# Six 20-byte tiles move from behind the attention tiles to ahead of the weights, which shifts the weights and most attention tiles by 192 bytes in SBUF

## The chip, the cores and the metric

The kernel runs on one core of a Trainium2 chip. The metric is the device time of one execution in microseconds (us). The kernel before was timed three times; a fourth execution was profiled.

## The reference

Block-causal attention over 8 batches and 8 heads, followed by a two-layer feed-forward net with a leaky ReLU:

```python
B, H, S, D = 8, 8, 576, 64                      # q, k, v: float32
scores = np.matmul(q, k.transpose(0, 1, 3, 2)) / np.sqrt(D)
scores = np.where(pos_i // 64 >= pos_j // 64, scores, -1e9)
scores = scores - np.max(scores, axis=-1, keepdims=True)
attn = np.exp(scores)
attn = attn / (np.sum(attn, axis=-1, keepdims=True) + 1e-09)
x = np.matmul(attn, v)                          # -> (4608, 512)
h = x @ w_in                                    # 512 -> 2048
out = np.maximum(0.01 * h, h) @ w_out           # 2048 -> 512, float32
```

## The kernel before

The kernel keeps everything on one core: attention for 64 heads, and the feed-forward net on the attention's rows, 256 tokens (a chunk) at a time, 18 chunks in all. Each matrix product of the feed-forward net is done three times with operands split into a high and a low part in the four-byte format fp32r, to keep float32 accuracy: high times high, high times low, low times high. The names end in h and l for the two parts.

**The first layer** (`ffn1`, matmuls of line 805). For a chunk and a pair `u` of 128-wide slices of the 2048 hidden columns there are 2 groups of 12 matmuls. In each the weights `wih` or `wil` are the stationary operand, 128 columns that are loaded into the array ahead of the matmul, and the activations `xh` or `xl` are the moving operand, 256 columns that stream through. 18 chunks, 8 pairs, 2 groups and 12 terms make 3456 matmuls, which write `p_h` in PSUM.

**The second layer** (`ffn2`, line 824). Here it is the other way round: the activations `gh` and `gl` are stationary, 128 columns, and the weights `woh` and `wol` are moving, 512 columns. For a chunk and a pair there are 2 groups of 6, in all 1728 matmuls, which write `p_o`.

**Attention.** The scores of a head (line 487) have queries `qs` as stationary and keys `kh`, `kl` as moving operand. The product with the values (line 641) has `vs` as stationary and the transposed probabilities `pth` (high) and `ptl` (low) as moving operand. The tiles `qs`, `kh` and `kl` exist twice, and successive heads take the one and the other (`z = i % 2`). Between the two products come the row maxima `nm` (VectorE, line 505), the exponentials with their row sums `sums` (ScalarE, line 514), the reciprocals `rec` (VectorE, lines 528 and 529), the division, and a transposition, which from the third batch on goes over DRAM (`turn`, `way`, `ptm`).

**Order.** A planner in the kernel (`class Plan`) simulates all operations with fixed costs, chooses an engine for those that can run on several, and writes them out; each engine then runs its list in order, with semaphores between engines. The planner's costs know nothing of addresses. The matmuls of the two layers are strewn between those of attention, so that TensorE has work while the softmax runs elsewhere; the last chunks run when attention is over.

**Memory.** The tiles of the pool `const` are laid out one behind the other in the order in which `fixed(...)` asks for them, each rounded up to a multiple of 32 bytes per partition. A tile's address is the same in each partition. In the kernel before, the first is `wih`, and the six tiles `nm`, `sums` and `rec` (two of each, 5 float32 values, 20 bytes per partition) come behind `vs` and ahead of `xr`, `g`, `gh`, `gl`, `xh`, `xl` and `ob`.

Of the kernel before, what the change touches and what calls it, by code (L numbers as in the profile page):

```python
# [9 lines left out]
F32 = mybir.dt.float32  # L10
# [7 lines left out]
P = 128  # L18
# [3 lines left out]
NT = 5  # L22
# [204 lines left out]
def attention_ffn(ctx: ExitStack, tc: tile.TileContext, qk: bass.AP, v: bass.AP, w_in: bass.AP, w_out: bass.AP, out: bass.AP):  # L227
# [33 lines left out]
    def fixed(shape, dt, name, n=None, pool=const):  # L261
        if n is None:
            return pool.tile(shape, dt, name=name)
        return [pool.tile(shape, dt, name=f"{name}{i}") for i in range(n)]
# [3 lines left out]
    def identity(pool):  # L268
        one = fixed([P, P], F32, "ident", None, pool)
        make_identity(nc, one)  # L270
        return one

    wih = fixed([P, ND, DFF], F32R, "wih")
    wil = fixed([P, ND, DFF], F32R, "wil")
    woh = fixed([P, NF, DM], F32R, "woh")
# [24 lines left out]
    kh = fixed([P, S], F32R, "kh", 2)  # L300
    kl = fixed([P, S], F32R, "kl", 2)
    vs = fixed([P, NT, 2 * D], F32R, "vs")
    nm = fixed([P, NT], F32, "nm", 2)
    sums = fixed([P, NT], F32, "sums", 2)
    rec = fixed([P, NT], F32, "rec", 2)
    for y in range(2):
        nc.gpsimd.memset(sums[y], 1.0)
    xr = [fixed([P, ND, S], F32, "xr0"), None]
# [603 lines left out]
```

## Time and profile before

| what | value |
|---|---|
| median of 3 runs | 1119.18 us (1118.76 to 1122.32) |
| the profiled execution, its own time | 1119.52 us |
| its span, first to last instruction | 1117.7 us |
| TensorE busy | 1083.7 us, 97% of the span, 6896 matmuls |
| weight loads busy (beside the matmuls) | 971.3 us, 87% |
| VectorE, ScalarE, GpSimd busy | 762.2, 708.3 and 475.5 us |
| granted TensorE clock, mean | 0.997 |

Busy time is the time in which at least one instruction of an engine is under way by the profile. The matmuls overlap each other in it (a matmul of the first layer is listed with some 0.28 us, and the next one starts about 0.115 us later), so what a matmul costs is read from one start to the next, not from its listed duration. The chain of waits, followed back from the last instruction, merges neighbouring pieces of one line and gives the length of each such stretch: divided by the number of its matmuls it gives the pace.

### The profile page before, as it was taken

To read this page: it belongs to the slowest core of one execution; us is meant where nothing else is said; L and a number is where in the kernel's file an instruction comes from. 1 tells how busy PE (TensorE), PEld (TensorE's weight loads), DVE (VectorE), ACT (ScalarE), POOL (GpSimd) and SP (SyncE) were. 2 spreads that over 40 slices of the span, in tenths; PEclk is the share of its full clock that TensorE was granted. 3 is DMA by queue.
4 is the path that set the end of the run, shared out by engine and by line. 5 is a ranking of instruction groups with operands and counts; after the bars stand their busy time and mean duration, and the time that the engine had idled before them with its cause. 6 is when DMAs were issued, how large, how long until landed. Compare 5 with 4: busy or idle time off the path is not lost.

```text
span 1117.7 us, 20595 instructions
## 1 busy us (share of the span) xinstructions
PE 1083.7 (97%) x6896; PEld 971.3 (87%) x6896; DVE 762.2 (68%) x2115; ACT 708.3 (63%) x1696; POOL 475.5 (43%) x501
## 2 busy tenths in 40 slices
PE   5799999999999999999999999999999999999998
PEld 4578788888889989999999998999989998999997
DVE  6998978879878777877666678787877776400000
ACT  7998767767777766655655566676677765322222
POOL 3444244545544444433443345455444445422221
PEclk9999999999999999999999999999999999999999
DMA  7766421157766656564445456656676655200000
GB/s 235 231 201 198 133 95 61 61 173 208 199 198 189 201 170 201 176 170 147 128 151 148 128 171 185 203 171 203 176 205 185 194 156 160 59 20 19 1 20 19
DMA packets 96810, 166.24 MB, mean 149 GB/s; under 512 B 10176, under 2 KB 79808, under 8 KB 96704
## 3 DMA queue, kind: packets, MB, share of 16 engines
q1 hardware_dynamic: 96704, 164.93, 50.0%
q8 instruction: 54, 0.88, 0.3%
q14 instruction: 52, 0.43, 0.1%
HBM read 111.41 MB, written 53.48 MB: 148 GB/s over the span
## 4 chain that ended last, share of the span: by engine, by line
PE 69%; DVE 16%; ACT 6%; DMA 4%; issue 2%; SPq 1%; POOL 0%; ACTq 0%; DVEq 0%; POOLq 0%
PE p_h L805 27%; PE p_o L824 27%; PE p_t L641 6%; PE p_s L487 6%; DVE nm L505 4%; ACT prow L514 4%; DVE turn L703 2%; DVE qs L464 2%; DMA way<-turn 2%; DMA ptm<-way 2%; PE p_t L568 2%; PE p_s L481 1%; DVE p_s L498 1%; DVE ptl L253 1%; SPq L720 1%
## 5 line engine op out<-in xcount | busy, mean ns | idle before, releaser
L805 PE MATMUL p_h<-xh,wih 128*128 128x256 f32 x1152 | 327.0, 284 | 1.6 <-DVE xh L244 1.6
L805 PE MATMUL p_h<-xl,wih 128*128 128x256 f32 x1152 | 323.1, 280 | 1.0 <-DVE xl L253 0.9
L805 PE MATMUL p_h<-xh,wil 128*128 128x256 f32 x1152 | 322.5, 280 | 0.0
L254 POOL TENSOR_TENSOR gl<-g,gh 128x512 fp32r<-128x512 f32 x110 | 149.4, 1359 | 368.2 <-ACT gh L243 317.7
L805 PEld LDWEIGHTS p_h<-xl,wih 128*128 128x128 f32 x1152 | 218.6, 190 | 11.6 <-DVE xl L253 1.4
L805 PEld LDWEIGHTS p_h<-xh,wih 128*128 128x128 f32 x1152 | 217.9, 189 | 11.8 <-DVE xh L244 1.8
L805 PEld LDWEIGHTS p_h<-xh,wil 128*128 128x128 f32 x1152 | 219.4, 190 | 0.0
L514 ACT ACTIVATE prow<-p_s,nm 128x192 f32<-128x192 f32 (+4 forms) x308 | 160.0, 525 | 74.1 <-DVE nm L505 73.4
L812 ACT ACTIVATE g<-p_h 128x512 f32<-128x512 f32 x144 | 86.0, 597 | 174.6 <-PE p_h L805 168.4
L824 PE MATMUL p_o<-woh,gh 128*128 128x512 f32 x576 | 183.1, 399 | 0.0
L824 PE MATMUL p_o<-wol,gh 128*128 128x512 f32 x576 | 179.7, 393 | 0.0
L824 PE MATMUL p_o<-woh,gl 128*128 128x512 f32 x576 | 179.1, 392 | 0.0
L703 DVE STREAM_TRANSPOSE turn<-prow 128x384 f32<-128x384 f32 (+3 forms) x384 | 143.9, 401 | 33.2 <-POOL prow L542 24.0
L542 POOL TENSOR_SCALAR prow<-prow,rec 128x320 f32<-128x320 f32 (+4 forms) x142 | 77.3, 557 | 148.7 <-DVE rec L529 106.7
L505 DVE TENSOR_REDUCE nm<-p_s 128x1 f32<-128x192 f32 (+4 forms) x308 | 137.4, 480 | 3.3
L824 PEld LDWEIGHTS p_o<-woh,gl 128*128 128x128 f32 x576 | 108.2, 188 | 24.8
L824 PEld LDWEIGHTS p_o<-wol,gh 128*128 128x128 f32 x576 | 108.2, 188 | 24.4
L544 ACT ACTIVATE prow<-prow,rec 128x192 f32<-128x192 f32 (+4 forms) x124 | 75.5, 614 | 48.6 <-DVE rec L529 48.4
L243 ACT CAST gh<-g 128x512 fp32r<-128x512 f32 x139 | 86.1, 620 | 22.0 <-PE p_o L824 20.5
L254 POOL TENSOR_TENSOR ptl<-ptm,pth 128x448 fp32r<-128x448 f32 x83 | 97.6, 1193 | 3.6 <-ACT pth L243 3.6
L243 ACT CAST pth<-ptm 128x448 fp32r<-128x448 f32 x191 | 94.4, 564 | 5.4 <-DMA ptm<-way 4.9
L824 PEld LDWEIGHTS p_o<-woh,gh 128*128 128x128 f32 x576 | 90.9, 188 | 3.6 <-issue 0.4
(81 smaller groups left out, 1655.0 us busy)
## 6 DMA issues: line engine op xcount, KB each, us to landing
way<-turn SPq DMA_DIRECT2D x192, 224.0 KB, 3.0
ptm<-way SPq DMA_DIRECT2D x192, 224.0 KB, 4.3
qk_in<-in_qk SPq DMA_DIRECT2D x56, 576.0 KB, 3.8
v_stage<-in_v SPq DMA_DIRECT2D x56, 160.0 KB, 2.3
out<-ob SPq DMA_DIRECT2D x35, 256.0 KB, 2.5
raw<-in_w_in SPq DMA_DIRECT2D x32, 256.0 KB, 3.3
raw<-in_w_out SPq DMA_DIRECT2D x32, 256.0 KB, 3.4
qk_in<-in_qk SPq DMA_DIRECT2D x8, 320.0 KB, 3.6
```

Of the source, the lines that this page charges most:

```text
L243: one = lambda: nc.scalar.copy(dst(), src())
L254: ("POOL", pool2(n), lambda: nc.gpsimd.tensor_sub(dst(), one(), two())),
L487: go = lambda ap=ap, cols=cols, kk=kk, k0=k0, k1=k1, first=first, last=last: nc.tensor.matmul(ap, qs[z][:, cols], kk[:, k0:k1], start=firs ...
L505: [("DVE", dve(kw[t]), lambda t=t, ap=ap, flat=flat: nc.vector.tensor_reduce(nm[z][: qn[t], t : t + 1], ap[: qn[t]], axis=AX.X if flat els ...
L514: nc.scalar.activation(o, ap[: qn[t]], AF.Exp, bias=nm[z][: qn[t], t : t + 1], scale=1.0, accum_out=sums[z][: qn[t], t : t + 1])
L542: ("POOL", pool1(kw[t]), lambda: nc.gpsimd.tensor_scalar(p(), p(), by, 1.0, op0=ALU.mult, op1=ALU.mult)),
L544: ("ACT", act(kw[t], True), lambda: nc.scalar.mul(p(), p(), by)),
L641: nc.tensor.matmul(to, vs[:, j, :], src, start=start, stop=stop)
L703: nc.vector.transpose(dst, src.rearrange("p (s b i) -> p s b i", b=4, i=32))
L805: nc.tensor.matmul(hh[:, i, :], w[:, d, f * P : (f + 1) * P], x[:, d, :], start=k == 0, stop=k == len(terms) - 1)
L812: add([("ACT", act(512), lambda: nc.scalar.activation(g, hh, AF.Prelu, alpha=0.01))], rank, [("h", z)], ["g"])
L824: nc.tensor.matmul(p_o[m], a[:, i, m * P : (m + 1) * P], w[:, 2 * u + i, :], start=u == 0 and k == 0, stop=u == NU - 1 and k == 5,)
```

## The change

The three lines that allocate the six small tiles stand ahead of those for the weights. Nothing else is touched.

```diff
         make_identity(nc, one)
         return one
 
+    nm = fixed([P, NT], F32, "nm", 2)
+    sums = fixed([P, NT], F32, "sums", 2)
+    rec = fixed([P, NT], F32, "rec", 2)
     wih = fixed([P, ND, DFF], F32R, "wih")
     wil = fixed([P, ND, DFF], F32R, "wil")
     woh = fixed([P, NF, DM], F32R, "woh")
...
     vs = fixed([P, NT, 2 * D], F32R, "vs")
-    nm = fixed([P, NT], F32, "nm", 2)
-    sums = fixed([P, NT], F32, "sums", 2)
-    rec = fixed([P, NT], F32, "rec", 2)
     for y in range(2):
         nc.gpsimd.memset(sums[y], 1.0)
```

In the built programs every instruction of every engine stands in the same place, with the same shape, before and after; only addresses differ. Six tiles of 32 bytes make 192 bytes, by which everything between the old and the new place moves up. What lies behind the old place stays. The start of a tile within a line of 512 bytes (its address modulo 512) is then:

| tile | role on TensorE | before | after |
|---|---|---|---|
| `wih`, `wil` | stationary, first layer | 384 | 64 |
| `xh`, `xl` | moving, first layer | 64 | 64 |
| `gh`, `gl` | stationary, second layer | 64 | 64 |
| `woh`, `wol` | moving, second layer | 384 | 64 |
| `qs`, `kh`, `kl`, heads with z = 0 | scores | 384 | 64 |
| `qs`, `kh`, `kl`, heads with z = 1 | scores | 128 | 320 |
| `pth` | moving, values | 384 | 64 |
| `ptl` | moving, values | 64 | 64 |
| `vs` | stationary, values | 384 | 64 |
| `prow0_1` to `prow0_4`, `qk_in0` | transposition, loads | 384 | 64 |
| `xr`, `g`, `ob`, `turn`, `ptm`, `v_stage` | copies and transfers | 64 or 320 | the same |
| `nm`, `sums`, `rec` | softmax | 384 to 32 | the same |

Slices of `wih`, `wil`, `woh`, `wol`, `xh`, `xl`, `gh`, `gl` and `vs` that a matmul reads start at multiples of 512 bytes within their tile, so the table holds for them too. All of these starts are multiples of 32 bytes, those of the large tiles multiples of 64.

## Prediction

> **What bounds the kernel.** I read the head of the page first, then the chain that ended last, then the timeline of TensorE.
>
> ```profile
> span 1117.7 us, 20595 instructions
> PE 1083.7 (97%) x6896; PEld 971.3 (87%) x6896; DVE 762.2 (68%) x2115; ACT 708.3 (63%) x1696; POOL 475.5 (43%) x501
> PEclk9999999999999999999999999999999999999999
> PE 69%; DVE 16%; ACT 6%; DMA 4%; issue 2%; SPq 1%; POOL 0%; ACTq 0%; DVEq 0%; POOLq 0%
> ```
>
> TensorE (PE) is busy 97% of the span at the full granted clock, and 69% of the chain is its matmuls. From 250 us on it has no gaps worth naming, and every other engine waits for it or works beside it. I therefore ask one question of the change: does a matmul follow its predecessor sooner or later when its operands start elsewhere? In the stretch from 440 to 640 us the chain is made of matmuls alone, and a count of the two layers' matmuls in the same window gives their mean pace:
>
> ```profile
> by line: PE p_o L824 41.5%; PE p_h L805 40.9%; PE p_s L487 9.1%; PE p_t L641 8.7%
> ...
> 440.00:640.00 200.00, 90.52 (x705) 89.72 (x706) 1.00 0.51 148
> ...
> 440.00:640.00 200.00, 91.62 (x360) 63.91 (x360) 1.00 0.51 148
> ```
>
> The first row is the chain in that window by line; the other two are the window's matmuls of line 805 (705) and of line 824 (360), with busy time and count, then the weight loads, the clock, DMA. First layer: 40.9% of 200 us is 81.8 us, over 705 matmuls 116.0 ns each. Second layer: 41.5% is 83.0 us, over 360 matmuls 230.6 ns each. These two means, times 3456 and 1728, are 400.9 and 398.5 us, together 71% of the time; the change moves one operand of every one of these 5184 matmuls.
>
> **How steady that pace is.** The chain's merged stretches show that identical matmuls do not always run alike:
>
> ```profile
> 446.53 0.53 PE p_s L487 x4
> 447.06 1.37 PE p_o L824 x6
> 448.43 1.41 PE p_h L805 x12
> 449.85 1.39 PE p_o L824 x6
> ...
> 454.40 1.12 PE p_s L487 x8
> ...
> 461.07 0.53 PE p_s L487 x4
> ...
> 468.94 1.12 PE p_s L487 x8
> ...
> 753.15 5.65 PE p_h L805 x48
> ...
> 1062.93 2.75 PE p_o L824 x12
> 1065.68 2.75 PE p_h L805 x24
> ```
>
> Columns: start, length, line, number of matmuls. The first layer runs at 5.65 / 48 = 117.7 ns per matmul in one stretch and at 2.75 / 24 = 114.6 in another. The second runs at 1.39 / 6 = 231.7 and at 2.75 / 12 = 229.2. Inside the quick stretch the starts one by one are
>
> ```profile
> 1066.22 0.28 PE L805 MATMUL p_h<-xh,wih 128*128 128x256 f32 x1
> ...
> 1068.15 0.28 PE L805 MATMUL p_h<-xh,wil 128*128 128x256 f32 x1
> 1068.26 0.39 PE L824 MATMUL p_o<-woh,gh 128*128 128x512 f32 x1
> ```
>
> with 18 first-layer matmuls from the first of these rows to the last: 2.04 us / 18 = 113.3 ns. So the first layer has a quick pace of 113.3 and a slow one of 117.7, and the mean of 116.0 lies between. Address and shape are the same in both, so the pace is set by how the streams of weight load and matmul fall against each other in time. This is the only place where I see a price that the addresses could touch.
>
> **The change part by part.** It removes and adds no instruction, moves none in any engine's list, adds no wait and touches no queue. What is left is where operands start.
>
> 1. *First layer, stationary operand.* `wih` and `wil` go from 384 to 64 in the 512-byte line, `xh` and `xl` stay at 64. Before, weights and activations start 320 bytes apart in the line, afterwards alike. Bounds: all matmuls at the quick pace give 3456 x (116.0 - 113.3) = 9.3 us less; all at the slow pace give 3456 x (117.7 - 116.0) = 5.9 us more.
> 2. *Second layer, moving operand.* `woh` and `wol` go from 384 to 64, `gh` and `gl` stay at 64. Bounds: 1728 x (230.6 - 229.2) = 2.4 us less, 1728 x (231.7 - 230.6) = 1.9 us more.
> 3. *Attention.* Queries and keys move together, so what lies alike there stays alike; `pth` and `vs` also move together, and `ptl`, which stays, becomes like `vs`. I take 0: the pair that changes is priced in the rows below at 0 to 5 ns for 280 matmuls, at most 1.4 us.
> 4. *Loads into `qk_in0`* (every second head in the first two batches and all heads after). The transfer is issued ahead and takes 3.8 us at the median:
>
> ```profile
> qk_in<-in_qk SPq DMA_DIRECT2D x56, 576.0 KB, 3.8
> ```
>
> A head takes about 14.5 us in the window above (scores start at 439.86, 454.40 and 468.94 by the chain's rows), which covers a transfer much slower than this. 0.
> 5. *VectorE, ScalarE, GpSimd* on shifted tiles: they hide under TensorE (68%, 63% and 43% busy), and the small tiles keep their place in the line. 0.
>
> For the value between the bounds of points 1 and 2 the trace has pairs that already lie alike. The scores have keys and queries at 384 and 384 for one head, at 128 and 128 for the next. Four of them, 288 columns each, take 0.53 us both at 446.53 and at 461.07, and eight take 1.12 us at 454.40 and at 468.94: where in the line the pair starts (256 bytes further) changes nothing that these rows can show. Their pace is 0.53 / 4 = 132.5 ns, that is 0.460 ns per column, and 117.7 / 256 is also 0.460: a pair that lies alike runs at the slow pace of a pair that does not. But four matmuls are the start of a group, and the first layer too starts slowly:
>
> ```profile
> 1075.15 0.28 PE L805 MATMUL p_h<-xh,wih 128*128 128x256 f32 x1
> ...
> 1075.63 0.28 PE L805 MATMUL p_h<-xl,wih 128*128 128x256 f32 x1
> ...
> 1076.54 0.62 PE L824 MATMUL p_o<-woh,gh 128*128 128x512 f32 x2
> ```
>
> Its first four matmuls take 0.48 us, 0.469 ns per column, the other eight 0.91 us, 0.444. So like against like position, pairs that lie alike are no slower, and at most 2% quicker for four matmuls. The second comparison is the product with the values, where the stationary `vs` (384) meets `pth` (384, alike) and `ptl` (64, 320 bytes apart as in the first layer), in listed durations:
>
> ```profile
> L641 PE MATMUL p_t<-ptl,vs 128*128 128x512 f32 x104 | 43.8, 421 | 0.1
> L641 PE MATMUL p_t<-pth,vs 128*128 128x512 f32 x104 | 43.3, 416 | 0.0
> ...
> L641 PE MATMUL p_t<-ptl,vs 128*128 128x256 f32 x48 | 13.5, 282 | 0.0
> L641 PE MATMUL p_t<-pth,vs 128*128 128x256 f32 x48 | 13.5, 280 | 0.0
> ...
> L805 PE MATMUL p_h<-xh,wih 128*128 128x256 f32 x1152 | 327.0, 284 | 1.6 <-DVE xh L244 1.6
> L805 PE MATMUL p_h<-xl,wih 128*128 128x256 f32 x1152 | 323.1, 280 | 1.0 <-DVE xl L253 0.9
> ```
>
> The unlike pair is 5 ns (512 columns) and 2 ns (256 columns) longer. Two kinds of first-layer matmul whose operands lie the same way differ by 4 ns in the same listing, merely by their place in the group, so I read the 2 to 5 ns as place too.
>
> The sum is therefore 0 for each point, with the bounds 9.3 + 2.4 + 1.4 = 13.1 us down and 5.9 + 1.9 = 7.8 us up. The profiled execution took 1119.52 us, 1.8 us more than its span and 0.3 us more than the median of the runs, 1119.18. Forecast: 1119.2 us for the median. No change means within 0.3%, 3.4 us, about what a measurement of this kernel can tell (its three runs spread by 3.6 us).
>
> The two paces are the row; a rule stands against them. The Trainium skill, page "TensorE: Matmul & The Clock Gate", section "Step-by-step: what each phase is for", says that TensorE reads moving operand and weights through two independent SBUF ports, so that loading the next weights takes nothing from the running matmul. By it, how the two lie to each other is worth exactly 0 us and both bounds fall away; it speaks against the change, and raises my chance for no change. The trace agrees only in part: with the ports free of each other a group of equal matmuls should have one pace, and the rows give 113.3 and 117.7 ns.
>
> **The rivals.**
>
> *Faster: the group settles at once.* If lying alike ends what makes the streams disturb each other, the start of each group and the slow stretches go, and both layers run at 113.3 and 229.2 ns: 9.3 + 2.4 us, 1107.8 us. For it: the mean lies nearer to the slow pace (2.7 ns above the quick one, 1.7 below the slow one), so there is more to win than to lose, and the two `ptl` rows point this way (2 ns on 3456 and 5 ns on 1728 matmuls would be 15.5 us, 1104.0). Against it: the scores lie alike and do not run at 0.443 ns per column.
>
> *Slower: the streams lock in the slow pace.* Weight load and matmul now start at the same offset, and if each step of the load meets the matmul's step in the same place, every group stays at 117.7 and 231.7 ns: 5.9 + 1.9 us, 1127.3 us. It decides once more than 43% of what could be lost is lost (3.4 of 7.8 us). For it: the scores' 0.460 ns per column, equal to the slow pace. Against it: the same pace heads each group of the unlike pair as well.
>
> *A part of either.* The means could shift by less than 3.4 us: this counts as no change.
>
> **How the numbers follow.** No change, because addresses at this grain do not matter or the two paces mix as before: 0.46. Faster by the first rival, in whole or large part: 0.31. Slower by the second: 0.23. The two rivals end near 1107.8 and 1127.3, and most of a partial effect lies inside; I take 1107 to 1127, which leaves out the 15.5 us reading of `ptl`, a wholly new pace and a full lock a little beyond the bound, together under 2 in 10. The likeliest case alone is 1116 to 1122.5.
>
> **What would show it.** Right: the stretches of line 805 in the chain again show both 113 and 117.7 ns, with 116.0 and 230.6 as means from 440 to 640 us. The faster rival: all long stretches of line 805 at 2.72 us per 24, the first four of a group included. The slower one: the last chunks, after attention, at 2.83 us per 24 instead of 2.75. Wrong altogether would be a pace outside 113.3 to 117.7, which would mean that the common part of the pace, and not only its spread, hangs on addresses.

## The result and the profile after

The changed kernel is slower: 1129.79 us median of 7 runs (1127.29 to 1132.70) against 1122.08 us of the kernel before on the same chip (1116.27 to 1123.68), ratio 1.0077 with a 95% interval from 1.0053 to 1.0100. The forecast of no change was wrong, and the median lies 2.8 us above the range. The kernel before took 2.9 us more in these runs than the 1119.18 us from which the forecast started; against its own base the change costs 7.7 us. The profiled execution took 1128.09 us with a span of 1126.3 us, 8.6 us longer than before.

The head of the page and its chain, after:

```profile
span 1126.3 us, 20595 instructions
PE 1094.0 (97%) x6896; PEld 981.6 (87%) x6896; DVE 760.7 (68%) x2115; ACT 708.4 (63%) x1696; POOL 473.7 (42%) x501
...
PE p_h L805 30%; PE p_o L824 29%; PE p_t L641 7%; PE p_s L487 6%; ACT prow L514 0%; DVE nm L505 0%; DVE xr L610 0%; ACT g L812 0%; ACT xr L243 0%; ACT g L243 0%; DVE p_s L498 0%; DVE xr L661 0%; ACT gh L243 0%; ACTq L243 0%; ACTq L514 0%
```

TensorE is busy 10.3 us longer, with the same instructions at the same clock, and idle 1.7 us less (34.0 us before, 32.3 after), which makes the 8.6 us of the span; the other engines' busy time is as before or a little less. The stages tell where. Busy time by engine before 250 us and from there to the end, first of the kernel before, then after (after the length of the stretch: busy time and count of TensorE, weight loads, VectorE, ScalarE and GpSimd, then the granted clock, the DMA share and GB/s):

```profile
0.00:250.00 250.00, 225.07 (x1366) 189.16 (x1366) 210.94 (x613) 196.05 (x529) 105.81 (x146) 0.99 0.50 154
250.00:1118.00 868.00, 858.68 (x5532) 782.15 (x5530) 551.24 (x1502) 512.21 (x1169) 369.69 (x355) 1.00 0.51 147
```

```profile
0.00:250.00 250.00, 225.11 (x1375) 189.86 (x1376) 211.02 (x618) 197.15 (x532) 106.10 (x148) 0.99 0.50 155
250.00:1127.00 877.00, 868.88 (x5522) 791.76 (x5521) 549.72 (x1498) 511.21 (x1166) 367.57 (x354) 1.00 0.50 145
```

In the first 250 us, where TensorE also waits for others, its busy time stays at 225.1 us. After that its busy time grows by 10.2 us. The window from 440 to 640 us of the kernel after, read as in the prediction (chain by line, then the count of line 805, then of line 824):

```profile
by line: PE p_h L805 41.6%; PE p_o L824 41.0%; PE p_s L487 8.9%; PE p_t L641 8.7%
...
440.00:640.00 200.00, 91.93 (x696) 90.44 (x696) 1.00 0.50 145
...
440.00:640.00 200.00, 90.51 (x355) 63.30 (x356) 1.00 0.50 145
```

First layer: 83.2 us over 696 matmuls, 119.5 ns each, before 116.0. Second layer: 82.0 us over 355, 231.0 ns, before 230.6. The first layer has 2988 of its matmuls after 250 us; 3.5 ns on each is 10.5 us, enough for the whole loss. (Line 805's own busy time in that part goes from 385.1 to 395.0 us, 9.9 us more; line 824's grows by 0.9 us.) The chain's long stretches show that this is no shift between the two paces seen before, but a third one:

```profile
756.49 5.75 PE p_h L805 x48
...
984.53 5.75 PE p_h L805 x48
990.28 2.75 PE p_o L824 x12
...
1073.33 2.87 PE p_h L805 x24
```

5.75 / 48 = 119.8 ns and 2.87 / 24 = 119.6 in each of these stretches, where the kernel before has stretches at 114.6 and at 117.7 ns. One group of the last chunks in the timeline:

```profile
1077.43 0.28 PE L805 MATMUL p_h<-xh,wih 128*128 128x256 f32 x1
1077.54 0.28 PE L805 MATMUL p_h<-xl,wih 128*128 128x256 f32 x1
1077.66 0.28 PE L805 MATMUL p_h<-xh,wil 128*128 128x256 f32 x1
...
1078.74 0.28 PE L805 MATMUL p_h<-xh,wil 128*128 128x256 f32 x1
1078.86 0.40 PE L824 MATMUL p_o<-woh,gh 128*128 128x512 f32 x1
```

The first matmul is followed after 0.11 us; the other eleven take 1.32 us, 120 ns each. The group of the kernel before in the prediction started slowly and then settled at 113.3. That holds beyond these rows: of the 233 first-layer runs of 12 matmuls or more from 250 us on, taken from the fifth start to the eleventh, 151 settle at 113 to 114 ns and 82 at 118 before, and all 233 at 119 to 120 after.

### The profile page after: what moved, and what is told of

Same layout as the page of the kernel before. It is cut to its first block, busy times and chain, and to the rows that moved or that the text cites. A ratio compares the mean times of both kernels' runs of the same rounds, so it can differ in the third digit from the quotient of the medians.

```text
span 1126.3 us, 20595 instructions
## 1 busy us (share of the span) xinstructions
PE 1094.0 (97%) x6896; PEld 981.6 (87%) x6896; DVE 760.7 (68%) x2115; ACT 708.4 (63%) x1696; POOL 473.7 (42%) x501
## 4 chain that ended last, share of the span: by engine, by line
PE 72%; ACT 0%; DVE 0%; issue 0%; ACTq 0%
PE p_h L805 30%; PE p_o L824 29%; PE p_t L641 7%; PE p_s L487 6%; ACT prow L514 0%; DVE nm L505 0%; DVE xr L610 0%; ACT g L812 0%; ACT xr L243 0%; ACT g L243 0%; DVE p_s L498 0%; DVE xr L661 0%; ACT gh L243 0%; ACTq L243 0%; ACTq L514 0%
## 5 line engine op out<-in xcount | busy, mean ns | idle before, releaser
L805 PE MATMUL p_h<-xl,wih 128*128 128x256 f32 x1152 | 326.4, 283 | 1.0 <-DVE xl L253 0.9
L805 PE MATMUL p_h<-xh,wil 128*128 128x256 f32 x1152 | 326.7, 284 | 0.0
L805 PEld LDWEIGHTS p_h<-xh,wih 128*128 128x128 f32 x1152 | 220.2, 191 | 11.8 <-DVE xh L244 1.8
```

The lines of the kernel that those rows point to most:

```text
L805: nc.tensor.matmul(hh[:, i, :], w[:, d, f * P : (f + 1) * P], x[:, d, :], start=k == 0, stop=k == len(terms) - 1)
```

## The experiments

The theory after the result: in the first layer the weight load of the next matmul runs beside the matmul that streams, both read SBUF, and the pace hangs on the distance between their start addresses (weights minus activations), with some period. Rivals: the weights' own place in the line counts; or something else that moved (small tiles, attention tiles, transfers). In all kernels below the distance is given modulo 512: before 320, after 0. The second layer, where the activations are loaded and the weights stream, has the same distance with the other sign.

**First set: period, or own place.** Four layouts. `d256`: the change, and one of the six large attention tiles (`kl1`, 2304 bytes) also ahead of the weights.

```diff
+    nm = fixed([P, NT], F32, "nm", 2)
+    sums = fixed([P, NT], F32, "sums", 2)
+    rec = fixed([P, NT], F32, "rec", 2)
+    kl1 = fixed([P, S], F32R, "kl1")
     wih = fixed([P, ND, DFF], F32R, "wih")
...
-    kl = fixed([P, S], F32R, "kl", 2)
+    kl = [fixed([P, S], F32R, "kl0"), kl1]
```

> Weights start 256 bytes behind the activations in the 512-byte line (320 against 64). Two bands: if the pace hangs on the distance modulo 128 or 256, this is the changed kernel again: first layer 119.4 ns, second 231.5 ns, +0.7% against before. If it hangs on the distance modulo 512 (only alike is bad): first layer 116 ns or less, within 0.3% of before or quicker. If the weights' own place decides: any pace.

Measured: ratio 1.0076 (1.0049 to 1.0104) to the kernel before, the loss of the change once more. First layer 41.6% of 200 us over 696 matmuls, 119.5 ns; long stretches as after the change:

```profile
475.56 4.32 PE p_h L806 x36
580.08 2.87 PE p_h L806 x24
```

So 256 bytes more of distance change nothing, and "alike within a line of 512 bytes" is not what counts.

`d064`: the kernel before with `kl1` alone ahead of the weights.

> Weights 64 bytes behind the activations (128 against 64). Distance modulo 128 or 256: the same residue as before (320), so first layer 116.0 ns, second 230.6 ns, within 0.3% of before. Distance modulo 512: a pace of its own, near that of alike if nearness counts (119 ns). Weights' own place: 128 is the same modulo 256 as 384 before, so 116 ns as well.

Measured: ratio 1.0022 (1.0004 to 1.0041). First layer 41.6% over 717, 116.0 ns. Its stretches have the pattern of the kernel before, quick and slow in the same places:

```profile
758.85 5.65 PE p_h L806 x48
984.54 5.46 PE p_h L806 x48
1027.24 2.75 PE p_h L806 x24
```

The interval of its time lies just above 1 all the same. Its runs also had a lower granted clock, 0.991 in the mean against 0.993 of the kernel before beside it, so the 0.2% can't be put down to the layout.

`d448`: `nm` and `sums` ahead of the weights, `rec` in its old place.

> Weights at 0, activations at 64: distance 448. Modulo 128 this is 64 as before: 116.0 and 230.6 ns, within 0.3% of before. Modulo 256 it is 192, a residue neither kernel has: then a pace of its own is possible, between 113.3 and 120 ns. Modulo 512 likewise.

Measured: ratio 1.0057 (1.0023 to 1.0090). First layer 41.5% over 707, 117.4 ns; second 40.2% over 343, 234.4 ns. Residue 192 is another pace than residue 64, so the period is not 128. Together with the two equal pairs (0 and 256, 64 and 320) it is 256 bytes, as far as these pairs show.

`d320_moved`: the kernel before with an unused tile of 128 bytes ahead of everything.

```diff
+    fixed([P, 32], F32, "gap")
     wih = fixed([P, ND, DFF], F32R, "wih")
```

> The kernel before with 128 unused bytes ahead of the weights: weights at 0, activations at 192, their distance 320 as before. If only the distance counts: the same time as before within 0.3%, 116.0 and 230.6 ns. If the start of the weights or of the activations in the line counts by itself: another pace; as weights at 0 are shared with the run at distance 448, the two would then be alike.

Measured: ratio 1.0005 (0.9984 to 1.0026), first layer 41.5% over 716, 115.9 ns. Everything moved and nothing happened; with weights at 0 this kernel and `d448` differ by 1.5 ns in the first layer. The weights' own place is out as the cause.

**Second set: which layer, and the other distances.** `second_only`: the three lines stand between `wil` and `woh`.

```diff
     wil = fixed([P, ND, DFF], F32R, "wil")
+    nm = fixed([P, NT], F32, "nm", 2)
+    sums = fixed([P, NT], F32, "sums", 2)
+    rec = fixed([P, NT], F32, "rec", 2)
     woh = fixed([P, NF, DM], F32R, "woh")
```

> The small tiles stand between wil and woh: only the second layer's weights (and the attention tiles) come to lie like the activations, the first layer's stay 320 bytes apart. If each layer pays for the distance of its own two operands: first layer 116.0 ns as before, second 231.6 ns as changed, and most of the loss is gone: below +0.3%. If something else moved with the small tiles (their own place, the attention tiles): first layer at 119.4 ns as well, +0.7%.

Measured: ratio 1.0041 (1.0024 to 1.0057), half of the loss, somewhat more than expected. The window:

```profile
by line: PE p_o L824 41.6%; PE p_h L805 40.9%; PE p_s L487 8.8%; PE p_t L641 8.7%
...
440.00:640.00 200.00, 90.75 (x704) 89.75 (x705) 1.00 0.51 146
...
440.00:640.00 200.00, 91.91 (x360) 63.99 (x360) 1.00 0.51 146
```

First layer 116.2 ns, second 231.1: the pace follows each layer's own distance. But in the last chunks the first layer, whose addresses are those of the kernel before, now runs at its slow pace throughout:

```profile
1023.07 2.83 PE p_h L805 x24
1067.84 2.83 PE p_h L805 x24
```

That is 117.9 ns against 114.6 before. Counted as above, 62 of the 233 runs settle at 113 to 114 ns and 171 at 118, where it was 151 and 82. Attention has ended in these last chunks, so among TensorE's operands there only the second layer's weights lie elsewhere: what the second layer's group leaves behind bears on which of its two paces the first layer's group settles at.

`d384` (`nm` ahead of the weights), `d352` (one of the six small tiles ahead) and `d288` (32 unused bytes behind `vs` in the kernel before):

> Distance 384, that is 128 modulo 256, the residue no run has yet. If nearness to alike is what costs, this is the quickest: first layer 113.3 to 115 ns, second 229 ns, up to 0.9% faster than before. If pace goes smoothly from residue 64 (116.1 and 231.1 ns) to 192 (117.6 and 233.9 ns): between them, 116.9 and 232.5 ns, +0.3%.

> Distance 352, 96 modulo 256: half a step of 64. If the grain is 64 bytes, this is like residue 64 or 128, 116.1 ns. If it is 32 bytes or finer: between the paces of 64 and 128, a pace of its own.

> The kernel before with 32 unused bytes ahead of the activations: distance 288, 32 modulo 256. Smooth in the distance: between alike (119.4 ns) and residue 64 (116.1 ns), so near 117.8 ns and +0.3%. Grain of 64 bytes: the pace of 0 or that of 64, 119.4 or 116.1 ns.

Measured: 1.0110 (1.0084 to 1.0136), 1.0099 (1.0076 to 1.0122) and 1.0074 (1.0053 to 1.0095). Residue 128, the farthest from alike, is not the quickest but nearly the slowest (119.3 ns): neither of the two bands expected for it came, and nearness to alike is no measure. `d352` has a pace of its own (118.1) between its neighbours, and `d288` 118.2, near the smooth guess, though its time is more than twice the +0.3% expected, as the second layer slowed too. Steps of 32 bytes matter. In `d288` the weights, the queries, keys and `vs` stay where they are in the kernel before, so a loss of this size comes about without any of these tiles moving.

**Third set: nothing moved but the load's start.** `w_back_after` is the changed kernel with one edit in the first layer: the load reads 128 columns that begin 48 columns (192 bytes) earlier, save for the first of the 16 slices of the hidden columns, which can't begin earlier. The kernel then multiplies with other weights, so its output is not the reference's; only the address is of interest.

```diff
+                f0 = max(0, f * P - 48)
                 nc.tensor.matmul(
-                    hh[:, i, :], w[:, d, f * P : (f + 1) * P], x[:, d, :], start=k == 0, stop=k == len(terms) - 1
+                    hh[:, i, :], w[:, d, f0 : f0 + P], x[:, d, :], start=k == 0, stop=k == len(terms) - 1
```

> The changed kernel, every tile in its place, but the first layer's weight loads read 48 columns (192 bytes) further back, so with other weights than the reference's (15 of 16 slices; the first stays). Their distance to the activations is then 64 modulo 256, as before. If the pace hangs on where the weight load starts against the moving operand: first layer 116.3 ns, second 232 ns as changed, time within 0.3% of before, or up to 0.4% above as with the second layer's tiles alone. If it hangs on anything else that moved (attention tiles, small tiles, transfers): 119.4 ns and +0.8% stay.

Measured: ratio 1.0032 (1.0014 to 1.0050) to the kernel before. The window:

```profile
by line: PE p_o L825 40.9%; PE p_h L806 40.6%; PE p_t L641 9.4%; PE p_s L487 9.2%
...
440.00:640.00 200.00, 90.03 (x696) 88.82 (x696) 1.00 0.52 149
```

116.7 ns, near the 116.3 expected. `w_back_before` is the same edit with 16 columns in the kernel before.

> The kernel before, every tile in its place, but the first layer's weight loads read 16 columns (64 bytes) further back (wrong weights in 15 of 16 slices). Distance 256, so 0 modulo 256. Same theory: first layer 119.2 ns, about 9 us in the part after 250 us, +0.8%, with nothing allocated elsewhere. Rival: 116.2 ns and the time of before.

Measured: ratio 1.0107 (1.0078 to 1.0136). The window:

```profile
by line: PE p_h L806 42.0%; PE p_o L825 39.7%; PE p_t L641 9.5%; PE p_s L487 8.8%
...
440.00:640.00 200.00, 92.66 (x705) 91.06 (x703) 1.00 0.52 151
```

119.1 ns, as expected. With every tile in its place, starting the weight load elsewhere takes more than half of the loss away in the one kernel and makes it in the other.

The slice that keeps its address is a control within the same execution. In `w_back_before`, a first-layer group of that slice starts at 1077.07 us, and the group of the next slice, whose loads are shifted, follows without a gap:

```profile
1077.77 0.28 PE L806 MATMUL p_h<-xh,wih 128*128 128x256 f32 x1
...
1078.45 0.28 PE L806 MATMUL p_h<-xh,wih 128*128 128x256 f32 x1
1078.57 0.28 PE L806 MATMUL p_h<-xl,wih 128*128 128x256 f32 x1
...
1079.89 0.63 PE L825 MATMUL p_o<-woh,gh 128*128 128x512 f32 x2
```

The last six matmuls of the slice that stayed take 0.68 us, 113.3 ns each. From the second matmul of the shifted slice on, eleven take 1.32 us, 120 ns each. In all its 15 groups after 250 us the slice that stayed settles at 113 to 118 ns here, the other fifteen at 119 to 120; in `w_back_after` it is the other way round, 119 to 120 for the slice that stayed and 113 to 118 for the others.

That settles the cause of the first layer's pace: the distance between the start of the weight load and that of the streaming operand. The small tiles, the attention tiles and the transfers have no part in this pace that these runs could show. Of the loss in time, 0.3% stays in `w_back_after` and 0.4% in `second_only`. In both the second layer's weights and the attention tiles lie as in the changed kernel. The last chunks of `second_only` show a part that comes with the second layer's weights; for the rest these runs don't tell the second layer from the attention tiles.

`d416` (`nm` and one `sums` ahead) and `d480` (all but one `rec` ahead) complete the distances:

> Distance 416, 160 modulo 256, not yet run. Between residues 128 (119.1 ns) and 192 (117.6): about 118.3 ns first layer, +0.7 to 1%. A residue quicker than 64 would show as less than 116 ns.

> Distance 480, 224 modulo 256, not yet run, the last multiple of 32. Between residues 192 (117.6 ns) and 0 (119.4): about 118.5 ns first layer, +0.7%. A residue quicker than 64 would show as less than 116 ns.

Measured: 1.0122 (1.0081 to 1.0163) and 1.0072 (1.0050 to 1.0095). The expected first-layer paces, 118.3 and 118.5 ns, took them to lie between their neighbours; with 119.8 and 116.9 they lie outside, `d416` above and `d480` below. Neither is quicker than 116 ns. All residues, with the paces of the window from 440 to 640 us (chain share of the line times 200 us over the line's count):

| distance modulo 256 | kernel | first layer, ns | second layer, ns | ratio to before |
|---|---|---|---|---|
| 0 | after; `d256` | 119.5; 119.5 | 231.0; 230.8 | 1.0077; 1.0076 |
| 32 | `d288` | 118.2 | 233.3 | 1.0074 |
| 64 | before; `d064`; `d320_moved` | 116.0; 116.0; 115.9 | 230.6; 230.5; 230.6 | 1; 1.0022; 1.0005 |
| 96 | `d352` | 118.1 | 233.3 | 1.0099 |
| 128 | `d384` | 119.3 | 231.7 | 1.0110 |
| 160 | `d416` | 119.8 | 233.9 | 1.0122 |
| 192 | `d448` | 117.4 | 234.4 | 1.0057 |
| 224 | `d480` | 116.9 | 232.6 | 1.0072 |

The shares are rounded to 0.1%, which leaves some 0.3 ns open between two paces of the first layer and 0.6 between two of the second. The paces come from a window at full granted clock; the ratios also hold differences of the clock between runs. The 23 runs of the kernel before beside the first set go from 1117.90 us at a clock of 0.995 to 1130.07 at 0.984, and the runs of `d480` have 0.991 in the mean, those beside them 0.995. So the paces are the firmer columns.

The kernel before has the quickest residue of the eight in both layers; no version here beats it.

## Why the prediction was wrong

**The bound (held).** TensorE's pace from start to start was the right quantity: its 10.3 us more of busy time, less the 1.7 us of idle time that went, are the whole change.

**Point 1, first layer (failed).** The step that failed is its upper bound. I took the slow pace of the trace, 117.7 ns, as the worst that another address could do, since both paces occur with the same addresses. The new distance has a pace of its own, 119.5 ns in the window and 120 when settled; the step was sized +5.9 us at most and measured 10.5. A pace outside 113.3 to 117.7 was what the prediction named as the sign of being wrong altogether. Paces of one layout say nothing of the range over layouts.

**The value between the bounds (failed).** I read from the scores that the place in the line does not matter, because pairs 256 bytes further took the same time. Both operands had moved together there, so their distance was the same, and 256 bytes is a whole period besides: the test was blind twice. And I compared the heads of groups, four matmuls against four. In the changed kernel the head is not the dear part: its first four matmuls take 0.47 us (1077.43 to 1077.90), before 0.48; the loss is in the settled eight that follow.

**Point 2, second layer (held here).** +0.4 ns, 0.7 us, inside its bounds. The bounds themselves were too narrow: distances 96 and 192 give 233.3 and 234.4 ns against the 231.7 that I took for the slowest.

**Points 3 to 5 (held).** Lines 487 and 641 have 8.9 and 8.7% of the window over 128 and 100 matmuls, 139.1 and 174.0 ns each, before 137.9 and 174.0. Counted from start to start over the whole trace from 250 us on, the scores cost 1.8 ns more each, 1.0 us in all, and the values 0.7 ns less, 0.3 us: together below the 1.4 us of the bound, though not nothing. VectorE's busy time fell by 1.5 us; the large `qk_in` loads still land in 3.8 us.

**The rule of the Trainium skill** (page "TensorE: Matmul & The Clock Gate", section "Step-by-step: what each phase is for": weights and moving operand come through two independent ports) had raised my chance for no change. The measurement decides against the consequence for this kernel, that how the two lie to each other is worth 0 us: the start of the weight load alone moves the first layer's pace from 119.5 to 116.7 ns in the one kernel and from 116.0 to 119.1 in the other. Whether there are two ports no run here shows.

**The rivals.** The slower one named the mechanism, groups that settle in a slow step because load and stream start alike, and its 7.8 us came near the 7.7 us between the medians, but that is luck: it is a sum of 5.9 and 1.9 us for the two layers, which measured 10.5 and 0.7, with 1.7 us of idle time to set against them. It had 0.23. The faster one, with the more, had as its best argument the listed durations of `ptl` against `pth`; they are modelled ends, and they pointed the wrong way.

**What stays open.** Why the period is 256 bytes, why residue 64 is best and 160 worst, what makes a group settle at one of several paces, and how much of the 0.3 to 0.4% that stays without the first layer's distance is the second layer's. That the reads of load and stream disturb each other is the reading that fits; the runs show only that their distance sets the pace. A kernel in which no load runs beside a matmul was not tried.

## What to carry to other kernels

In this kernel, where TensorE is the bound and each matmul has its own weight load in four-byte data, the distance between the two operands' start addresses modulo 256 bytes is worth up to 1.2% of the time, and a new tile ahead of one of them changes it unless its size is a multiple of 256 bytes. Whether a kernel of another shape pays as much was not tried. Fix it on purpose, and when an unrelated edit costs 0.5 to 1%, look at the addresses first. A pace is read from starts in settled stretches, not from the listed durations or the head of a group.

## What the runs showed of the hardware

- The pace of 256-column matmuls with a 128-column weight load each, by distance modulo 256 bytes: 115.9 to 119.8 ns in the mean, and the same within the rounding for distances 256 apart (0 and 256; 64 and 320).
- With one layout a run of equal matmuls settles at one of two paces, 113.3 or 117.7 ns; with only the second layer's weights lying elsewhere, the last chunks go from the quick one to the slow one. At distance 0 it settles at 120.
- Moving both operands by 128 bytes together changed the first layer by 0.1 ns in the window, within the rounding.
